# Infini-attention beside a Fourier mixing: where SyncE issues the row loads of the next head group, and where the transposing transfer

## The chip, the cores and the metric

The kernel runs on one core of a Trainium2 chip. The metric is the device time of one execution in microseconds (us), as the median of repeated runs. A core has five engines that matter here: TensorE (PE, matmuls; PEld is its weight load), VectorE (DVE), ScalarE (ACT), GpSimd (POOL) and SyncE (SP). In this kernel SyncE does nothing but issue the transfers (DMAs), in the order of the program.

## The reference, cut to what matters

Two independent results stand side by side in the output. A is an attention with a compressive memory over 2048 rows of width 576, with 32 heads of 18 and four segments of 512 rows; B is a Fourier mixing, two matrix products along the width and two along the sequence.

```python
# A, for each of the 4 segments
p = softmax(qs @ ks.T * scale + causal_mask)      # 512 x 512 per head
a_dot = p @ vs
a_mem = (phi(qs) @ M) / (phi(qs) @ z + 1e-6)
o = g * a_mem + (1 - g) * a_dot
M, z = M + phi(ks).T @ vs, z + phi(ks).sum()
out_A = o_all @ wo
# B
a, b = x @ dft_hid_re.T, x @ dft_hid_im.T
out_B = dft_seq_re @ a - dft_seq_im @ b
```

## The kernel before, in words

Full precision is kept by splitting: a float32 operand becomes a rounded high part and the low remainder, and a product becomes three matmuls.

There are three stages. The first (lines 435 to 479) goes through the segments: `project_qk` and `project_v` make queries, keys and values, `lookup` and `accumulate` read and write the memory. Queries and keys are stored in DRAM (`qd`, `kd`) as three bf16 parts each, values as `vd`. The second stage holds two streams at once. `attention()` (line 805) does the softmax attention of A as 68 steps `p` of eight pieces; after each piece it yields a share of time (`SLOTS`), and the loop at line 867 fills that share on TensorE with matmuls of `dense()` (line 573), which is B: 16 tiles of `hidden` and 16 of `sequence` for the real part, then the same for the imaginary part. The third stage multiplies the attention's output by `wo`.

The instructions of every engine are issued in the order in which this program emits them; nothing reorders them later. `later(n, fn)` (line 82) puts a call `n` ticks ahead, and a tick falls after each piece, so that a load is issued that many pieces later.

Heads go in groups of four. `stack_load(G)` (line 420) brings the rows of group `G` from DRAM: twelve transfers, six into `qs` and six into `ks`, each for one of the bf16 parts, spread over three ticks (`each=2`), or over six ticks for the first group (`each=1`), and `lag` ticks later the group's values, `vst`. There are four buffers for the rows of a group. In `attention()` group `G` is loaded by the step `p = 2G - 2`, and its first scores (`s_fill`, line 673, the matmul at line 664) stand at the opening of step `p = 2G`. A matmul of scores reads all the parts of a head, so it needs all twelve transfers.

Even and odd heads take different ways. For an even head the row maxima are found first, transposed by TensorE (`maxima_transpose`, line 719), written to DRAM (`md`) and read back into three more rows of `qs` (line 725); then scores are computed a second time in transposed form (`t_fill`, line 727) with the maxima as part of the product. For an odd head the exponentials `f` are split into `hl` by ACT (line 700), POOL and DVE (line 704), and one transposing transfer (`f_turn`, line 706, the DMA at line 709) turns `hl` into `ptt`, with two buffers, which `pv` (line 765) multiplies with the values. There is one such transfer per step.

SyncE waits at each issue for what the transfer needs. Each transfer signals on one of eight semaphores, taken in turn, and the issue of a transfer also waits for the one that used its semaphore before, eight places back.

Before the change `stack_load(p // 2 + 1)` is called in the first piece of an even step, and `f_turn` at the end of the last piece of each step. On SyncE the twelve rows so stand behind the transposing transfer of the odd step before, with the store `md` between them, and the load of `md` into `qs` stands behind the rows. The first group's call stands at `n == 6` of the last segment's loop over the projections (line 462), so that its last pair is issued in the last of the four value blocks.

The quoted functions follow.

## Time and profile before

| | |
|---|---|
| median of 3 runs | 1030.98 us (1029.33 to 1032.97) |
| the profiled execution | 1030.27 us, its span 1028.5 us |
| VectorE, ScalarE, GpSimd busy | 69%, 70%, 61% |
| transfers of SyncE's queue | 73.5% of the 16 engines' span, 192.81 MB |
| transposing transfers | 64 |
| row loads | 384, of 72 KB each |

A line of the page's list of groups or waits names the line of the kernel, the engine and the tile that is written and read (`s<-ks,qs` is a matmul into `s`). "A <- B" in a list of waits says that A waited for B. In a timeline the first figure is the start in us from the start of the span and the second the length; an idle time ahead of the instruction stands in brackets with what ended it; x2 says that two are merged. For a transfer the timeline shows the time that SyncE spends on the issue, not the landing; the chain of waits shows the time to the landing where a landing is part of the chain. In a table of windows each row gives the window, its length, the busy time of PE, PEld, DVE, ACT and POOL, the granted clock of TensorE (1.00 is full), the DMA engines' busy share and GB/s.

### The profile page before, as it was taken

The page shows a single profiled execution, that of the slowest core. Times are in us where ns is not written, and L with a number is a line of the kernel's source. Part 1 is how long each engine was busy: PE and PEld are TensorE (multiplying, and loading weights), DVE is VectorE, ACT ScalarE, POOL GpSimd, SP SyncE. Part 2 cuts the span into 40 slices and gives each one's busy share as a digit, 9 for nine tenths or more (in the row PEclk, how much of TensorE's full clock was granted, in tenths as well). Part 3 has the DMA queues.
Part 4 walks back from the last instruction along what each step waited for, and adds up shares of the span by engine and source line. Part 5 has one row for each costly group of instructions (what it writes and reads, how often), then busy time and mean ns, then how long its engine had stood idle before and what let it go on. Part 6 is the DMA issues. An engine that isn't in the chain of part 4 may idle for free.

```text
span 1028.5 us, 25886 instructions
## 1 busy us (share of the span) xinstructions
PE 1007.7 (98%) x9464; PEld 942.5 (92%) x9464; DVE 705.9 (69%) x1903; ACT 715.0 (70%) x1654; POOL 624.2 (61%) x668
## 2 busy tenths in 40 slices
PE   9999999989999999999999999999999999999998
PEld 7989989889999999998998999999999889999998
DVE  6645557563677777778888777777777778885442
ACT  6657575653777787877878788877677777876333
POOL 2657575775666677676766867666667567666000
PEclk9999999998999999999999999999999999999999
DMA  7516243375568887898998987689998899977574
GB/s 250 186 65 204 88 159 147 128 242 151 154 157 190 199 207 197 210 218 193 221 215 194 217 188 182 164 202 226 224 217 195 202 242 234 235 176 182 156 209 137
DMA packets 287743, 194.46 MB, mean 189 GB/s; under 512 B 210496, under 2 KB 242816, under 8 KB 287616
## 3 DMA queue, kind: packets, MB, share of 16 engines
q1 hardware_dynamic: 287616, 192.81, 73.5%
q8 instruction: 74, 1.21, 0.5%
q14 instruction: 53, 0.43, 0.1%
HBM read 106.84 MB, written 43.97 MB: 147 GB/s over the span
## 4 chain that ended last, share of the span: by engine, by line
PE 83%; DMA 7%; ACT 2%; POOL 2%; DVE 2%; SPq 2%; issue 1%; POOLq 0%; ACTq 0%; DVEq 0%
PE d L493 31%; PE qk L78 6%; PE s L664 6%; PE d L78 6%; PE qk L230 5%; PE v L78 4%; PE pv L780 4%; PE d L539 3%; PE d L540 3%; PE d L541 3%; DMA qs<-md 2%; PE pv L781 2%; PE m L314 2%; DMA ptt<-hl 2%; DMA ks<-kd 2%; PE look L339 1%
## 5 line engine op out<-in xcount | busy, mean ns | idle before, releaser
L670 DVE CUSTOM_DVE_ANT_0 s<-s,causal 128x128 f32<-128x128 f32 (+3 forms) x512 | 251.7, 498 | 119.9 <-PE s L664 108.6
L393 POOL TENSOR_TENSOR clo<-craw,chi 128x512 fp32r<-128x512 f32 x158 | 209.6, 1327 | 161.4 <-ACT chi L388 128.1
L493 PE MATMUL d<-wide,chi 128*128 128x288 f32 x1408 | 266.7, 306 | 0.0
L493 PEld LDWEIGHTS d<-wide,chi 128*128 128x128 f32 x1408 | 212.3, 189 | 1.3 <-issue 0.2
L493 PE MATMUL d<-wide,clo 128*128 128x288 f32 x704 | 178.0, 319 | 0.0
L664 PE MATMUL s<-ks,qs 108*128 108x128 bf16 (+3 forms) x512 | 134.2, 304 | 6.7 <-DMA ks<-kd 4.3
L704 POOL TENSOR_TENSOR hl<-pf,hl 128x768 f16<-128x768 f32 x64 | 110.2, 1723 | 48.5 <-ACT hl L700 39.8
L693 ACT ACTIVATE pf<-s,nb 128x128 f32<-128x128 f32 (+3 forms) x256 | 128.3, 527 | 6.2
L493 PE MATMUL d<-ab,chi 128*128 128x288 f32 x640 | 126.1, 306 | 0.0
L748 ACT ACTIVATE phi<-t 128x384 f16<-128x384 f32 x128 | 62.3, 487 | 83.7 <-PE t L745 83.7
L493 PEld LDWEIGHTS d<-wide,clo 128*128 128x128 f32 x704 | 119.0, 189 | 1.0
L388 ACT ACTIVATE chi<-craw 128x512 fp32r<-128x512 f32 x160 | 100.6, 630 | 8.1 <-DMA craw<-cT 3.3
L763 DVE TENSOR_TENSOR plo<-pf,phi 128x384 f16<-128x384 f32 (+1 forms) x128 | 105.0, 821 | 0.0
L749 ACT ACTIVATE pf<-t 128x384 f32<-128x384 f32 (+1 forms) x192 | 100.1, 521 | 3.8 <-PE t L738 3.7
L493 PEld LDWEIGHTS d<-ab,chi 128*128 128x128 f32 x640 | 98.5, 189 | 0.4
L700 ACT ACTIVATE hl<-pf 128x768 f16<-128x768 f32 (+1 forms) x128 | 87.4, 729 | 2.0
L539 PE MATMUL d<-wide,chi 128*128 128x288 f32 x256 | 85.6, 334 | 0.0
L493 PE MATMUL d<-ab,clo 128*128 128x288 f32 x320 | 84.9, 314 | 0.0
L540 PE MATMUL d<-wide,chi 128*128 128x288 f32 x256 | 76.5, 299 | 0.0
L541 PE MATMUL d<-wide,clo 128*128 128x288 f32 x256 | 76.4, 299 | 0.0
L763 POOL TENSOR_TENSOR plo<-pf,phi 128x384 f16<-128x384 f32 x64 | 61.3, 957 | 11.5 <-ACT pf L749 10.7
L704 DVE TENSOR_TENSOR hl<-pf,hl 128x512 f16<-128x512 f32 x64 | 62.9, 982 | 0.7 <-ACT hl L700 0.5
(196 smaller groups left out, 2522.8 us busy)
## 6 DMA issues: line engine op xcount, KB each, us to landing
craw<-cT SPq DMA_DIRECT2D x128, 256.0 KB
qs<-qd SPq DMA_DIRECT2D x192, 72.0 KB
ks<-kd SPq DMA_DIRECT2D x192, 72.0 KB
craw<-xtT SPq DMA_DIRECT2D x32, 320.0 KB
out<-y SPq DMA_DIRECT2D x31, 288.0 KB
vd<-vs SPq DMA_DIRECT2D x16, 440.0 KB
vst<-vd SPq DMA_DIRECT2D x32, 220.0 KB
qd<-p SPq DMA_DIRECT2D x16, 384.0 KB
```

The lines of the kernel that those rows point to most:

```text
L78: pe.matmul(o, a, b, start=n == 0, stop=n == len(terms) - 1)
L388: act.activation(hi, raw[:, :4], AF.Copy)
L393: engine.tensor_tensor(lo, raw[:, :4], hi.bitcast(F32), OP.subtract)
L493: pe.matmul(o[h], a, b[:, h * 288:h * 288 + 288], start=start, stop=stop)
L539: pe.matmul(o, xh[:, k], wl[k][:, cs], start=k == 0, stop=False)
L540: pe.matmul(o, xh[:, k], wh[k][:, cs], start=False, stop=False)
L541: pe.matmul(o, xl[:, k], wh[k][:, cs], start=False, stop=False)
L664: pe.matmul(o[:, c:c + w], q[:, i * P:w], k[:, :w], start=True, stop=True)
L670: dve.tensor_tensor_reduce(o[:, c:c + w], o[:, c:c + w], CAUSAL[0][:, L - w:], scale=scale, scalar=-LOWEST, op0=OP.add, op1=OP.min, accum_ ...
L693: act.activation(f[:, FIRST_COL[i]:FIRST_COL[i] + w], o[:, c:c + w], AF.Exp, bias=nb[:, i:i + 1], scale=-1.0)
L704: engine.tensor_tensor(hl[:, 1, a:b], f[:, a:b], hl[:, 0, a:b], OP.subtract)
L763: (pool if kind == 2 else dve).tensor_tensor(lo[:, a:b], f[:, a:b], hi[:, a:b], OP.subtract)
```

## The change

Three things are moved, and nothing is added or taken out.

- The first group's rows: the call moves from `n == 6` to `n == 4`, and with it the making of the first pair of buffers (and POOL's fill of one). The loads are issued two ticks sooner.
- The transposing transfer `f_turn` moves from the end of the last piece to the opening of the last but one.
- The rows of the next group are called right behind it, in the seventh piece of an even step instead of its first. The delay of the values' load goes from 39 to 33 ticks, so that it keeps its piece.

On SyncE the rows of a group now follow the transposing transfer of the even step and, for most groups, the load `vst`; the transposing transfer of the odd step comes after them. The maxima's store and load no longer have rows between or ahead of them. The orders of TensorE, VectorE and ScalarE stay the same, and POOL's but for the one fill.

```diff
-    def stack_load(G, lag=39, each=2):
+    def stack_load(G, lag=33, each=2):
...
-            if not more and n in (5, 6):
-                stacks(sr, n - 5)
+            if not more and n == 4:
+                stacks(sr, 0)
+                stack_load(0, 99, 1)
             if not more and n == 5:
                 c_load(0)
             if not more and n == 6:
-                stack_load(0, 99, 1)
+                stacks(sr, 1)
...
-            if p % 2 == 0:
-                stack_load(p // 2 + 1)
             if p % 2 == 0 and 0 < p <= NP:
                 maxima_transpose(p // 2 - 1)
...
             yield SLOTS[5]
+            odd(F_LAG + 1, f_turn)
+            if p % 2 == 0:
+                stack_load(p // 2 + 1)
             odd(V_LAG, pv)
...
             if p >= V_LAG:
                 pv_out(p - V_LAG)
-            odd(F_LAG + 1, f_turn)
             yield SLOTS[7]
```

## The prediction

> **What bounds the kernel now.** I read the page first, then the list of waits of TensorE, then the windows and timelines around the waits, last the chain of waits. The page says that TensorE is the bound:

> ```profile
> span 1028.5 us, 25886 instructions
> ...
> PE 1007.7 (98%) x9464; PEld 942.5 (92%) x9464; DVE 705.9 (69%) x1903; ACT 715.0 (70%) x1654; POOL 624.2 (61%) x668
> ```

> Matmuls fill 1007.7 of 1028.5 us. The change leaves TensorE's order as it is, so it can win only out of the 20.8 us that remain. The list of TensorE's waits divides them (engine, line, what it waited for, total us, times, longest):

> ```profile
> PE s L664 <- DMA ks<-kd: 4.3, 1, 4.3
> PE t L738 <- DMA qs<-md: 3.9, 6, 0.9
> PE pv L780 <- DMA ptt<-hl: 2.4, 2, 1.7
> PE s L664 <- DVE negm L670: 2.3, 3, 0.9
> ...
> PE trm L721 <- POOL mb L717: 1.4, 1, 1.4
> ```

> Three are waits for SyncE's transfers, and each has its part of the change: the first group's rows (4.3 us, once), the maxima rows (3.9) and the transposing transfer (2.4), 10.6 us together. The other two rows are not touched.

> The first wait costs more than its length. In TensorE's timeline it stands ahead of the first scores, and the matmuls behind it run slow:

> ```profile
> 232.06 0.58 PE L664 MATMUL s<-ks,qs 108*128 108x512 bf16 x1 [4.34 <-DMA ks<-kd]
> ...
> 236.76 0.44 PE L540 MATMUL d<-wide,chi 128*128 128x288 f32 x1
> 237.00 0.44 PE L541 MATMUL d<-wide,clo 128*128 128x288 f32 x1
> ...
> 262.24 0.30 PE L540 MATMUL d<-wide,chi 128*128 128x288 f32 x1
> 262.37 0.30 PE L541 MATMUL d<-wide,clo 128*128 128x288 f32 x1
> ```

> The same pair of matmuls starts 0.24 us apart here and 0.13 us apart later. The windows (PEclk is the third figure from the end) show why, and that a wait of 1.7 us, which is the longest one at L780, does not do this:

> ```profile
> 225.00:237.50 12.50, 8.16 (x46) 7.80 (x45) 5.51 (x13) 3.44 (x9) 6.00 (x6) 0.75 0.71 230
> ...
> 825.00:837.50 12.50, 10.81 (x117) 10.04 (x117) 8.93 (x28) 7.43 (x18) 6.94 (x10) 1.00 0.98 239
> ```

> The clock was at half speed for the 5.3 us from 232.1 to about 237.4, which costs 5.3 x (1 - 0.13/0.24) = 2.4 us.

> **Part one, the first group's loads two steps sooner: minus 6.7 us.** Nothing is added; a fill of ks on POOL and twelve row loads (DMAs) move up past the kd stores. SyncE's timeline before:

> ```profile
> 217.84 0.38 SPq L378 DMA_DIRECT2D craw<-xtT  x1
> 218.28 1.11 SPq L88 DMA_DIRECT2D qs<-qd  x1
> ...
> 228.24 0.35 SPq L88 DMA_DIRECT2D ks<-kd  x1
> ```

> The last ks row goes out at 228.24, behind the stores of the third value block. In the new order the last pair stands behind the craw load of 217.84, so it goes out near 219 and should land four to five us later, well before TensorE is free for the first scores (232.06 - 4.34 = 227.7). The 4.3 us and the slow clock's 2.4 us both go. On POOL the fill goes ahead of one subtraction that only a kd store waits for, and those rows are read many groups later. I name nothing that is late next. If the cover fails, no more than the 6.7 us comes back.

> **Part two, the transposing transfer a piece sooner, ahead of the rows: minus 6.3 us.** It is one issue on SyncE per step, and it is long:

> ```profile
> L709 SPq DMA_TRANSPOSE ptt<-hl x64: 3013/3814/5378, 272.1 to 943.7; - x64
> ```

> One period of two steps in SyncE's timeline, then VectorE's two ends of hl in it, then TensorE's scores that open a period:

> ```profile
> 484.10 3.06 SPq L709 DMA_TRANSPOSE ptt<-hl  x1
> ...
> 488.78 0.80 SPq L88 DMA_DIRECT2D qs<-qd  x2
> 489.63 0.83 SPq L88 DMA_DIRECT2D ks<-kd  x2
> 490.55 0.30 SPq L88 DMA_DIRECT2D md<-mt  x1
> ...
> 494.27 0.34 SPq L88 DMA_DIRECT2D od<-og  x1
> ...
> 495.46 0.69 SPq L88 DMA_DIRECT2D ks<-kd  x2
> 496.20 0.75 SPq L88 DMA_DIRECT2D qs<-md  x1
> ...
> 497.53 0.59 SPq L432 DMA_DIRECT2D vst<-vd  x1
> 498.23 4.00 SPq L709 DMA_TRANSPOSE ptt<-hl  x1
> ...
> 505.35 4.53 SPq L709 DMA_TRANSPOSE ptt<-hl  x1
> ```

> ```profile
> 493.23 1.76 DVE L704 TENSOR_TENSOR hl<-pf,hl 128x512 f16<-128x512 f32 x1
> ...
> 504.51 0.69 DVE L704 TENSOR_TENSOR hl<-pf,hl 128x512 f16<-128x512 f32 x1
> ```

> ```profile
> 488.53 0.38 PE L664 MATMUL s<-ks,qs 108*128 108x512 bf16 x1
> ...
> 509.02 0.38 PE L664 MATMUL s<-ks,qs 108*128 108x512 bf16 x1
> ```

> The transfer of 505.35 starts 0.15 us after its data (504.51 + 0.69 = 505.20): it waits for VectorE, and an earlier place in the order gives it nothing. The one of 498.23 had its data at 494.99 and stood 3.2 us behind the rows and the maxima. That half comes sooner, and the late pv (2.4 us) goes. The maxima row at 496.20 stands behind the twelve rows; without them it goes out some 3 us sooner, and the 3.9 us at L738 go too. What it newly waits for is its own store, which the rows used to cover, and behind that wait stand a craw load and the next transposing transfer.

> **Part three, the rows behind the transposing transfer: plus 25 us.** This is the disputed term. No work is added (twelve loads of 72 KB per group, as before), but they lose their lead. Before, the rows of the group that starts at 509.02 went out from 488.78 to 496.15, and 495.83 + 4.1 (below) leaves nine us after landing. Now they start when the transfer that has its data at 494.99 is issued. The chain of waits gives what a landing takes (start, us, what):

> ```profile
> 489.63 4.58 DMA ks<-kd
> ...
> 496.20 4.07 DMA qs<-md
> ...
> 717.00 8.15 DMA ptt<-hl
> ...
> 794.35 3.15 DMA md<-mt
> ```

> A transfer takes one of eight semaphores in turn, and its issue waits until the one eight places ahead has landed: the ks row of 489.63 lands at 494.21, and the eighth issue behind it, od, goes out at 494.27. So, in that period: transposing transfer at 495.1, off SyncE after 4.0 (499.1), vst 0.6 (499.7), eight rows at 0.4. The ninth waits for vst to land, taken at 4 us like the rows (503.1), the last ones for the first rows, so the twelfth goes out near 504.5 and lands 4.1 to 4.6 us later: 508.6 to 509.1, against 509.02. On its own that is a stall of about 0.1 us. But the transposing transfer need not start at 495.1. SyncE now holds, between two such transfers, the rows and two craw loads at the pace of the landings, then the other transposing transfer, then the maxima's store and the wait for it (3.15 us), with only od and a craw load to fill it. That makes it late by 0 to 2 us; I take 1.0, the middle, since neither end has a nearer row. The stall is then 1.1 us per group. It counts in the stretches with a period of 20.5 us (509.02 - 488.53); the hidden products have longer ones, and there the transfers have room (GB/s is the last figure, the DMA share stands before it):

> ```profile
> 385.00:551.00 166.00, 163.79 (x1775) 152.96 (x1773) 131.24 (x372) 131.84 (x307) 111.96 (x114) 1.00 0.88 208
> 593.00:665.00 72.00, 72.00 (x750) 68.27 (x749) 54.17 (x166) 58.72 (x152) 49.11 (x58) 1.00 0.74 178
> 707.00:898.00 191.00, 185.03 (x2002) 172.24 (x2001) 147.59 (x443) 142.49 (x328) 127.67 (x132) 1.00 0.93 221
> ```

> With shares of 0.88 and 0.93 there is little room to catch up. Some 23 of the 32 groups lie in such stretches (all but the first few and those beside the second hidden products): 23 x 1.1 = 25 us. The ends: 0 if every chain comes out under 14 us (a short transposing issue of 3.0 us alone gives 1.0 back), and 23 x 1.9 = 44 us if SyncE is late by most of the 2 us each time.

> [...]

> **The sum.** The profiled execution took 1030.27 us, 0.7 below the median of 1030.98. 1030.3 - 6.7 - 3.9 - 2.4 + 25 = 1042.3 us.

> **The rivals.** *First, on the other side: the rows land in time.* SyncE's one transposing issue in two is shorter when less is queued ahead of it (3.06 at 484.10, 4.00 at 498.23); each us there is a us of margin, and above 0.1 to 1.1 us of it the stalls end. For it: fewer transfers stand between the transposing one and the last row (md and od are gone). Against it: the DMA share. Then 1030.3 - 13.0 = 1017.3 us. *Second, the two cancel:* stalls of 0.6 us per group, 23 x 0.6 = 13: 1030 us. *Third, long stalls slow the clock as the first one did:* if the 11 groups of the later stretch, where the share is 0.93, each stall 4.3 us, they cost 4.3 + 2.4 each, 74 us: 1091 us. Against it: 4.3 us is more than twice the lateness that I allow. [...] *Fourth, that the change does not do what it says* holds for half of the transposing transfers, as shown; it is in the sum.

> **How the numbers follow.** Rows late, about 1042 us: 0.65. In time, 1017: 0.20. Cancelled, 1030: 0.11. Slow clock, 1091: 0.04. A measurement of this kernel can tell about 0.3% (3 us) from no change; so faster 0.20, same 0.11, slower 0.69. The range goes from 1016, the first rival less the spread of runs (1029.33 against the median of 1030.98), to 1061, the forecast with the upper end of the stalls (1017 + 44).

> **What would show it.** Right: the row of s at L664 waiting for qs or ks leads TensorE's waits with 15 us or more in over ten waits, none of them near 230 us; the waits for qs<-md and ptt<-hl are gone; PEclk is 1.00 from 225 us on. The maxima's load on SyncE follows its store by three us or more. Wrong: no such row at L664 (then the first rival, near 1017), or waits at L738 that stay (then md was not held by the rows). A wait at L664 near 230 us would refute part one. What would make the sum wrong is above all the pace of landings once the rows stand elsewhere, which no row of this profile shows.

## The result and the profile after

The changed kernel takes 1061.15 us (median of 4 runs, 1057.41 to 1064.64) against 1031.91 us before (4 runs): ratio 1.029, 95% interval 1.024 to 1.033. The profiled execution took 1057.41 us, 27.1 more than the one of before. It is slower, as forecast, by some two and a half times as much as forecast. Here and below, times and ratios leave out runs more than 1.5% above the fastest of their kernel; two of the kernels had such runs. The code below the change stands one line lower (L664 is now L665, L738 is L739). The page of the changed kernel gives span and engines:

```profile
span 1055.7 us, 25951 instructions
...
PE 1015.6 (96%) x9464; PEld 949.7 (90%) x9464; DVE 703.4 (67%) x1903; ACT 716.0 (68%) x1654; POOL 618.9 (59%) x668
```

TensorE's idle time has grown from 20.8 to 40.1 us, and the same matmuls take 7.9 us longer: 19.3 + 7.9 is the whole 27.2 us of the span. Both parts have their place. The list of TensorE's groups has one row for the scores; behind the bar stand busy time, ns of one, idle time ahead of them and what ended it:

```profile
L665 PE MATMUL s<-ks,qs 108*128 108x128 bf16 (+3 forms) x512 | 134.8, 306 | 31.4 <-DMA ks<-kd 8.1 <-DMA craw<-cT 7.1 <-DMA y<-yd 4.2
```

The row had 6.7 us before, 4.3 of them in the first group. Of the 31.4 us, 28.9 stand ahead of the first scores of 19 groups, in TensorE's timeline, 0.2 to 3.3 us each, 1.5 on the mean; no wait stands near 230 us. The releasers that the row names vary (a row, a chunk load, a y load, now and then ScalarE), but in 18 of the 19 groups the scores start within 0.5 us of the landing of the group's last row, as the trace's landings give it; the one left, at 558 us, is 0.2 us long. The waits for qs<-md and ptt<-hl are gone from TensorE's list. SyncE's own list of waits has a new row, which it had not before:

```profile
SPq L88 <- DMA md<-mt: 27.0, 25, 2.2
```

One period of SyncE's timeline, with VectorE's end of hl and TensorE's opening scores from theirs:

```profile
839.34 4.14 SPq L710 DMA_TRANSPOSE ptt<-hl  x1
843.54 0.58 SPq L432 DMA_DIRECT2D vst<-vd  x1
844.18 0.88 SPq L88 DMA_DIRECT2D qs<-qd  x2
...
849.26 0.80 SPq L88 DMA_DIRECT2D ks<-kd  x2
850.35 0.36 SPq L378 DMA_DIRECT2D craw<-cT  x1
850.89 4.90 SPq L710 DMA_TRANSPOSE ptt<-hl  x1
855.84 0.57 SPq L378 DMA_DIRECT2D craw<-cT  x1
856.51 0.34 SPq L88 DMA_DIRECT2D md<-mt  x1
```

```profile
838.57 0.69 DVE L705 TENSOR_TENSOR hl<-pf,hl 128x512 f16<-128x512 f32 x1
```

```profile
855.30 0.38 PE L665 MATMUL s<-ks,qs 108*128 108x512 bf16 x1 [1.05 <-ACT pf L694]
```

VectorE ends at 839.26, the transposing transfer starts 0.08 us later, the rows follow at once, and the last one lands at about 855.0: 15.7 us from the transfer's start, and 1 us too late. That is the chain of part three.

The longer matmuls come from the clock. Windows of the changed kernel, of 3.41 us (the DMA share passes 1 in windows as short as these):

```profile
828.60:832.02 3.42, 0.23 (x2) 0.23 (x3) 1.46 (x2) 2.72 (x6) 0.91 (x2) 1.00 1.24 211
832.02:835.43 3.41, 3.41 (x18) 3.26 (x17) 0.76 (x2) 0.99 (x2) 2.61 (x2) 0.50 1.01 185
872.98:876.39 3.41, 1.64 (x29) 1.44 (x28) 2.95 (x10) 2.87 (x8) 1.37 (x2) 1.00 1.23 224
876.39:879.80 3.41, 3.03 (x13) 2.97 (x13) 1.41 (x4) 1.62 (x4) 1.71 (x2) 0.50 1.06 184
804.72:808.13 3.41, 1.94 (x16) 1.73 (x15) 2.63 (x8) 0.00 (x0) 0.34 (x1) 1.00 1.05 252
808.13:811.54 3.41, 3.22 (x27) 2.96 (x26) 1.28 (x5) 2.99 (x7) 2.00 (x2) 1.00 1.33 269
```

With a stall of 3.30 us (it ends at 831.8) and one of 2.15 us (876.8) the clock stood at half for 3.41 us; with one of 1.47 us (807.7) it did not. Six such spells go with six stalls of 2.07 to 3.30 us, at 340.5, 449.7, 763.8, 832.0, 876.4 and 924.2 us. Before there was one, twice as long (231.15 to 237.98), at the first group's wait.

### The profile page after: what moved, and what is told of

It reads as the page before. It is cut to its first block, busy times and chain, and to the rows that moved or that the text cites. A ratio compares the mean times of both kernels' runs of the same rounds, so it can differ in the third digit from the quotient of the medians.

```text
span 1055.7 us, 25951 instructions
## 1 busy us (share of the span) xinstructions
PE 1015.6 (96%) x9464; PEld 949.7 (90%) x9464; DVE 703.4 (67%) x1903; ACT 716.0 (68%) x1654; POOL 618.9 (59%) x668
## 4 chain that ended last, share of the span: by engine, by line
PE 75%; DMA 10%; ACT 4%; SPq 4%; POOL 3%; DVE 2%; issue 1%; POOLq 0%; ACTq 0%; DVEq 0%
PE d L494 26%; PE qk L78 6%; PE d L78 6%; PE s L665 6%; PE qk L230 5%; PE v L78 4%; DMA ks<-kd 4%; PE d L540 3%; PE d L541 3%; PE d L542 3%; DMA craw<-cT 3%; PE pv L781 3%; DMA qs<-qd 2%; PE m L314 2%; SPq L88 2%; SPq L710 2%
## 5 line engine op out<-in xcount | busy, mean ns | idle before, releaser
L494 PEld LDWEIGHTS d<-wide,chi 128*128 128x128 f32 x1408 | 216.7, 192 | 1.3 <-issue 0.2
L665 PE MATMUL s<-ks,qs 108*128 108x128 bf16 (+3 forms) x512 | 134.8, 306 | 31.4 <-DMA ks<-kd 8.1
L388 ACT ACTIVATE chi<-craw 128x512 fp32r<-128x512 f32 x160 | 100.8, 631 | 26.0 <-DMA craw<-cT 16.8
L665 PEld LDWEIGHTS <-qs 108*128 108x128 bf16 x512 | 40.3, 98 | 50.4 <-issue 19.0
L540 PE MATMUL d<-wide,chi 128*128 128x288 f32 x256 | 84.4, 330 | 0.0
L541 PE MATMUL d<-wide,chi 128*128 128x288 f32 x256 | 75.7, 296 | 0.0
```

The source lines that it names most:

```text
L388: act.activation(hi, raw[:, :4], AF.Copy)
L494: pe.matmul(o[h], a, b[:, h * 288:h * 288 + 288], start=start, stop=stop)
L540: pe.matmul(o, xh[:, k], wl[k][:, cs], start=k == 0, stop=False)
L541: pe.matmul(o, xh[:, k], wh[k][:, cs], start=False, stop=False)
L665: pe.matmul(o[:, c:c + w], q[:, i * P:w], k[:, :w], start=True, stop=True)
```

## The experiments

Every ratio is against the kernel before on the same chip, with its 95% interval; a difference between two of the kernels is that of their ratios, in us of 1031. The first theory was that of the prediction: the rows have lost their lead, and SyncE's blocked wait for the maxima's store makes the transposing transfer ahead of them late. The rivals change with what the runs showed.

### The parts alone

*Part one alone* (the first group's loads sooner; the rest as before).

> The kernel before with part one alone: the first group's rows two steps sooner, all else as before. By the sum of the prediction the wait of 4.3 us at the first scores and the half clock behind it (2.4 us) go: 6.7 us less than before, ratio 0.9935, and the waits at L738 and L780 stay. If the first group's sooner loads only crowd the stores of kd and of the values, the time stays within 2 us of before and a wait of another kind stands near 230 us.

1026.83 us, 0.996 (0.995 to 0.998). Its page and its list of waits:

```profile
PE 1005.2 (98%) x9464; PEld 940.8 (92%) x9464; DVE 704.1 (69%) x1903; ACT 714.6 (70%) x1654; POOL 622.4 (61%) x668
```

```profile
PE t L739 <- DMA qs<-md: 6.8, 6, 2.6
```

The first wait is gone, and in the profiled run the clock never fell; without a half-clock spell the matmuls take 1005.2 us, 2.5 less than before (2.4 had been worked out). But the maxima's waits rose from 3.9 to 6.8 us, and some 4 us of the 6.7 remain.

*The transposing transfer a piece sooner alone*, the rows in their old place:

```diff
             yield SLOTS[5]
+            odd(F_LAG + 1, f_turn)
             odd(V_LAG, pv)
...
-            odd(F_LAG + 1, f_turn)
             yield SLOTS[7]
```

> The kernel before with part two alone: the transposing transfer a piece sooner in the order, the rows still called in the first piece of the even step. My theory (it is the rows' place that costs, not the transposing transfer's): half of these transfers wait for VectorE anyway, the other half stay behind the rows and the maxima; within 3 us of before, waits at the scores only the first one of 4.3 us. A rival, that the transposing transfer's sooner place holds up what follows it on SyncE (its issue waits for hl with everything behind it): 10 us slower or more.

1035.96 us, 1.005 (1.003 to 1.008): slower. In its list of waits the pv wait halved and the maxima's grew by more:

```profile
PE t L738 <- DMA qs<-md: 9.8, 9, 2.7
...
PE pv L780 <- DMA ptt<-hl: 1.2, 1, 1.2
```

### More lead for the rows, same place in the step

*Rows two steps sooner* in the changed kernel:

```diff
-            if p % 2 == 0:
+            if p in (0, 2):
                 stack_load(p // 2 + 1)
+            elif p == 3:
+                stack_load(3, 41)
+            elif p % 2 == 0:
+                stack_load(p // 2 + 2, 49)
```

> The changed kernel with the rows at the same place of the step but two steps (one group) sooner, so SyncE's order has the same pattern and the same load between the transposing transfers; only the lead grows by some 21 us. If the loss is the lost lead, the waits at the scores and the half clock behind them go, and so do those for the maxima and the transposing transfer: 13 us less than before, about 1018 us, ratio 0.987. If the loss is SyncE blocked by the wait for the maxima's store, or the order of the transfers on the DMA engines, both are still there, and the time stays over 1040 us, with the waits moved to the maxima or to ptt.

1051.1 us, 1.019 (1.016 to 1.023). No row is late any more, and yet only 10 of the 30 us come back. Its waits, TensorE's and ScalarE's:

```profile
ACT chi L388 <- DMA craw<-cT: 35.0, 19, 5.9
...
PE t L742 <- ACT mt L724: 13.4, 5, 3.8
...
PE s L665 <- ACT pf L694: 3.6, 3, 3.0
```

ScalarE waits for the other stream's chunk loads (16.8 us in the changed kernel), TensorE for ScalarE, and five half-clock spells stand in the trace. SyncE is still blocked 30.2 us for the maxima's store. So the lead is not the whole of it.

*Rows one step sooner*, behind the odd step's transfer, with the maxima behind them:

```diff
-            if p % 2 == 0:
+            if p in (0, 2):
                 stack_load(p // 2 + 1)
+            elif p % 2 and p > 1:
+                stack_load((p + 3) // 2, 41)
```

> The changed kernel, but the rows go behind the transposing transfer of the odd step, one step sooner: they gain 10 us of lead, and the maxima's store and load stand behind the rows again, with nothing long between. Theory (what costs is the place of the rows behind the even step's transfer: it leaves them no lead, and everything that SyncE issues behind them, the odd step's transfer, the maxima's store and the chunk loads of the other stream, comes late too): the waits at L665 for rows are gone, ScalarE waits for chunk loads for less than 8 us (16.8 in the changed kernel), the waits for the maxima are 4 to 10 us as with either other part alone, and the time is 1027 to 1037 us. Rival (the loss comes from the transposing transfer being issued sooner, or from the rows meeting it on the DMA engines, whichever of the two it is): 1045 us or more.

1069.54 us, 1.039 (1.036 to 1.042). The time is the rival's, the cause is neither's, for the maxima's waits grew:

```profile
PE t L739 <- DMA qs<-md: 29.3, 18, 4.7
```

All twelve rows now go out ahead of the maxima's store, whose landing SyncE then waits for with nothing to issue (71.0 us in its list). In the old order four rows go out first and the others while the store is under way.

*The maxima's load behind the even step's transfer*, so that SyncE isn't blocked for the store (`later(4, ...)` in `maxima_transpose` becomes `later(7, ...)`).

> The changed kernel with the maxima's load three pieces later, so that it stands behind the transposing transfer of the even step and SyncE no longer stands blocked for the maxima's store ahead of it (27 us in the changed kernel's list of SyncE's waits, 25 times). If that blocked wait makes the chain late (the second half of my part three), the transposing transfer and the rows start some 1 us sooner each time, and about 20 us of the 29 us of waits at the scores go, with new short waits for the maxima at L739: about 1040 us. If it is the lead alone, by far the most of the loss stays: 1055 us or more.

1078.27 us, 1.047 (1.044 to 1.050). The row waits fall to 2.9 us and the maxima's take their place:

```profile
PE t L739 <- DMA qs<-md: 43.4, 28, 2.9
```

### The maxima without the trip through DRAM

In four kernels the maxima rows go straight from their tile into qs, by two transfers in place of two (the rows of `mb` are put in the order head, part, tile for it):

```diff
-        later(1, dma, md[G], w)
-        later(4, dma, qs_bufs[G % 4][NPAIR:NPAIR + 3, 0:4:2], md[G].rearrange("(c h n) t -> c h (n t)", c=3, h=2))
+        for h in range(2):
+            later(1, dma, qs_bufs[G % 4][NPAIR:NPAIR + 3, 2 * h], w[12 * h:12 * h + 12])
```

*In the changed kernel:*

> The changed kernel, but the maxima rows go straight from their tile into qs by two transfers, with no trip through DRAM, so that SyncE never waits for their store (27.0 us in the changed kernel). Theory (the stall is a chain that runs from VectorE's end of hl through the transposing transfer, vst and the twelve rows to their landing; in the changed kernel that transfer starts within 0.1 to 1.1 us of its data, so the blocked wait adds little to it): the row waits at L665 fall by no more than 0.5 us each, 1045 to 1058 us. Rival (the blocked wait makes that transfer late by 1.0 us, as the prediction put it): the waits fall to about 0.5 us each, no half-clock spell is left, 1035 us or less.

1049.56 us, 1.018 (1.014 to 1.022): 11 us of the loss come back. The row waits, in the list of groups, fall by 5.8 us, and three half-clock spells are left of six:

```profile
L665 PE MATMUL s<-ks,qs 108*128 108x128 bf16 (+3 forms) x512 | 134.0, 304 | 25.6 <-DMA craw<-cT 7.4 <-DMA ks<-kd 5.7 <-ACT pf L694 4.1
```

*With the rows one step sooner:*

> The kernel with the rows one step sooner (1069.5 us; 29.3 us of waits for the maxima, 38.7 us of ScalarE's for chunks), with the maxima rows sent directly. Theory (there the maxima's store goes out only behind the twelve rows, and its trip, 4.2 us to land and 2.1 more for the load, is exposed): the waits at L739 fall below 8 us, 1030 to 1045 us. Rival (SyncE is crowded at that place, whichever transfers stand there): 1055 us or more.

1036.02 us, 1.006 (1.004 to 1.008), 34 us less than with the trip. Of its waits:

```profile
ACT chi L388 <- DMA craw<-cT: 46.2, 28, 4.1
...
PE t L740 <- DMA qs<-mt: 1.5, 2, 1.3
```

So the exposed trip of the maxima was most of the loss there. And the largest wait for chunks of these kernels, 46.2 us, goes with one of the shorter times: ScalarE's wait for chunks is no measure of the loss.

*With the rows two steps sooner:*

> The kernel with the rows two steps sooner (1051 us; no row late, but ScalarE waits 35 us for chunk loads and TensorE 20 us behind it), with the maxima rows sent directly. Theory (the chunk loads are late because SyncE stands blocked for the maxima's store, 30.2 us, and because the rows are issued in one run between the transposing transfers; the first share goes): ScalarE's waits for chunks fall to 10 to 25 us, 1030 to 1045 us. Rival (the blocked wait has no part in it): 1048 us or more. Second rival (it is all of it): 1028 us or less.

1045.0 us, 1.013 (1.009 to 1.017): the upper end of the theory's range, but ScalarE's waits for chunks did not fall (35.5 us), so the way that it named is not the one.

*In the old order, with part one:*

> The kernel before with the first group's rows sooner (1026.8 us), with the maxima rows sent directly. Theory (in the old order the trip of the maxima through DRAM is the tightest of SyncE's chains): the 6.8 us of waits at L739 are gone and nothing takes their place, 1017 to 1022 us. Rival (what stands behind the maxima in the order is as late): 1025 us or more.

1033.25 us, 1.003 (1.001 to 1.005), 7 us slower than with the trip. The maxima's waits are gone, pv waits 9.5 us for ptt instead, and in the later stretch the transposing issue takes 4.5 us on the mean in place of 4.1.

### The place of the rows, and the place of the scores

*Rows ahead of the even step's transfer*, three pieces sooner; all else as in the changed kernel:

```diff
             yield SLOTS[2]
+            if p % 2 == 0:
+                stack_load(p // 2 + 1, 36)
...
             odd(F_LAG + 1, f_turn)
-            if p % 2 == 0:
-                stack_load(p // 2 + 1)
             odd(V_LAG, pv)
```

> The changed kernel, with the transposing transfer where the change puts it, but the rows called three pieces sooner, so that they stand ahead of the even step's transfer in SyncE's order; the maxima's store and load stay ahead of them. Theory (the stalls come from the rows' place behind that transfer, 4.7 us of issue and its wait for VectorE): no row is late, the six half-clock spells are gone, and what is left is the transfer some 3 us behind its data, which pv has time for: 1022 to 1032 us. Rival (the rows anywhere between the maxima's load and the next store crowd SyncE, as with the rows two steps sooner): chunk loads late, 1040 us or more.

1040.69 us, 1.009 (1.006 to 1.012): 20 of the 30 us are back. The run whose profile was taken had no half-clock spell and took 1034.19 us, the other six 1040.0 to 1043.7 at a mean clock of 0.993 to 0.995 (1.000 in the profiled one), which speaks for some. Its waits, then, are those of the fastest run:

```profile
ACT chi L388 <- DMA craw<-cT: 23.6, 11, 4.5
...
PE pv L781 <- DMA ptt<-hl: 9.7, 9, 2.6
...
PE s L665 <- ACT pf L694: 6.9, 5, 3.1
```

No row is late (from the third group on the rows land 4.6 us or more ahead). The transfer, now behind the rows, is late instead.

*The opening scores one piece later on TensorE*, nothing moved on SyncE (`even(0, s_fill, 0)` goes from the first piece to the end of the second).

> The changed kernel with the scores that open a step computed one piece later on TensorE, behind the first two transposed ones: some 2 us more for the rows to land, nothing else moved. Theory (the chain from VectorE's hl to the last row's landing is too long by 0.2 to 3.3 us, 1.5 on the mean, and the longer stalls bring the half clock on): the row waits fall from 28.9 to under 8 us, at most one half-clock spell stays, 1028 to 1038 us. Rival (the chain closes on itself: what TensorE gains, VectorE's next hl takes, or the maxima become late): 1048 us or more.

1055.7 us, 1.023 (1.019 to 1.027): the rival. Its groups:

```profile
L665 PE MATMUL s<-ks,qs 108*128 108x128 bf16 (+3 forms) x512 | 133.3, 304 | 8.7 <-DMA ks<-kd 4.3 <-DMA craw<-cT 3.2 <-DVE negm L671 1.0
...
L739 PE MATMUL t<-qs,ks 111*128 111x128 bf16 x256 | 25.5, 223 | 9.3 <-ACT pf L694 9.3
```

The row waits fall as expected, but waits for ScalarE at L739 (9.3) and L742 (6.2) come up in their place, and the steps are hardly shorter: from 717 us on the groups start 22.3 us apart, 22.8 in the changed kernel and 21.1 before. That the chain from VectorE's hl to the rows to the scores to the next hl closes on itself is the rival's reading; it fits, but no run isolates it.

### The chunk loads off SyncE

In six kernels the chunk loads (`c_load`, from the sixth on) are issued by another engine, three times by ScalarE, three times by GpSimd:

```diff
-            dma(t[:, :k], src[at])
+            (act.dma_start if n > 4 else dma)(t[:, :k], src[at])
```

*ScalarE: the changed kernel; rows two steps sooner; the old order with part one.*

> The changed kernel with the chunk loads issued by ScalarE. Theory: the row waits at L665 get shorter by the 0.8 us that two chunk loads take between two transposing transfers, from 1.5 us each to 0.5 to 1.0, fewer half-clock spells (0 to 3 in place of 6), 1035 to 1048 us. Rival (the rows land late because of the DMA engines, not because of SyncE's order): 1055 us or more.

> The kernel with the rows two steps sooner (1051 us), but the chunk loads of the other stream (craw) are issued by ScalarE, a queue of their own. In the kernel with them on SyncE no row was late any more, yet ScalarE waited 35 us for chunks, up to 5.9 us at a time. Theory (those late chunks hold up ScalarE's exponentials and by them TensorE): the waits for chunks fall below 8 us, TensorE's waits at L742 and for pf (20 us together) to under 5, the clock stays at 1.00, and the time is 1025 to 1036 us. Rival (the load of SyncE or of the DMA engines as such, or the maxima behind the odd step's transfer): the waits move to the maxima or to ptt, 1043 us or more.

> The kernel before with the first group's rows sooner (1026.8 us), and the chunk loads issued by ScalarE. Theory: SyncE has 0.8 us less to issue per step, the maxima come sooner, the 6.8 us of waits for them fall below 3: 1020 to 1025 us. Rival (the 0.8 us per step on ScalarE, busy 70%, delay the exponentials by as much): 1027 us or more.

1099.25 us, 1.068 (1.065 to 1.072); 1100.25 us, 1.070 (1.065 to 1.075); 1112.11 us, 1.080 (1.075 to 1.084). All far slower: on the side of the rivals, and by more than either side had named. SyncE's waits in the last one:

```profile
SPq L88 <- DMA craw<-cT: 81.7, 40, 5.5
```

With part one alone this row has 3.1 us (10 times). The transfers at L88 neither read nor write a chunk, so SyncE here waits for semaphores that chunk loads signal on, and ScalarE now issues those at its own time. The test says nothing on late chunks; it was made again with GpSimd (`pool.dma_start`), where that wait comes to 0.5 us in the first kernel.

*GpSimd: the old order with part one; the changed kernel; rows two steps sooner.*

> The kernel before with the first group's rows sooner (1026.8 us), and the chunk loads issued by GpSimd, the engine that releases their buffers. With ScalarE as the issuer SyncE waited 82 us for chunk loads, whose semaphores its own transfers share (1112 us). Theory (what harmed there was that sharing, not the second queue as such; GpSimd's transfers have semaphores of their own): no wait of SyncE for a chunk is left, SyncE's issue has 0.8 us less per step, the waits for the maxima fall below 3 us, 1019 to 1026 us. Rival (two queues at once slow the transposing transfers, or GpSimd, busy 61%, is late with the low parts): 1040 us or more.

> The changed kernel with the chunk loads issued by GpSimd. Theory (rows and chunk loads are late together because both stand in one queue behind the transposing transfer; two chunk loads stand between that transfer and the last row): ScalarE's waits for chunks (16.8 us) are gone, the row waits fall by the 0.8 us of two issues each, 1036 to 1050 us. Rival (as with ScalarE as the issuer): 1055 us or more.

> The kernel with the rows two steps sooner (1051 us, no row late, ScalarE waits 35 us for chunks), the chunk loads issued by GpSimd. Theory (the late chunks are what holds up ScalarE and by it TensorE): no waits for chunks, 1024 to 1036 us. Rival (the chunk loads' lateness is only where the wait is booked, and GpSimd or the transposing transfers take their place): 1045 us or more.

1077.37 us, 1.047 (1.040 to 1.054); 1100.74 us, 1.067 (1.064 to 1.070); 1065.54 us (two runs), 1.036 (1.028 to 1.044). The rival's time each time. Waits of the first one, TensorE's:

```profile
PE pv L781 <- DMA ptt<-hl: 31.6, 11, 7.0
...
PE t L739 <- DMA qs<-md: 16.3, 13, 4.0
```

and SyncE's in the second, where the blocked wait has nearly tripled:

```profile
SPq L88 <- DMA md<-mt: 77.1, 30, 5.2
```

The chunks are not what is late now (ScalarE waits 9.3 us for them in the second, 16.8 in the changed kernel; in the first 4.1 us, 1.9 with part one alone), but everything that SyncE issues is: in the first, from 330 to 950 us, a row lands 4.5 us after its issue (median; 3.6 with part one alone), the maxima's store 4.8 (3.2), the transposing transfer 7.8 (6.1). No run here tests apart why they take longer. The first kernel's other rival, GpSimd late with the low parts, is not seen: its part of hl ends 2.9 us ahead of VectorE's in the median, 2.4 with part one alone.

### A version that might beat both

*The maxima's store ahead of the rows, their load ahead of the last four*, in the old order with part one (the calls of `maxima_transpose` and `stack_load` change places, `later(4, ...)` becomes `later(3, ...)`).

> The kernel before with the first group's rows sooner (1026.8 us, 6.8 us of waits for the maxima), and the maxima's store put ahead of the twelve rows, their load ahead of the last four. Theory (in the old order the tightest chain is the maxima's trip, and the rows beside it have nine us to spare): the store goes out 1.6 us sooner, the load some 2 to 3 us, the waits at L739 are gone, 1018 to 1023 us. Rival (the load then stands blocked for its store, and the transposing transfer behind it and the rows comes late instead): 1025 us or more.

1028.37 us, 0.997 (0.995 to 0.999): the maxima's waits are gone, pv waits 7.0 us for ptt instead. Part one alone, 1026.83 us, can't be told from it by these intervals; no other of these kernels is as fast.

## Why the prediction was right and wrong

**The sign was right, and so was the place of the waits.** The scores that open a group wait for rows that have lost their lead, no wait stands near 230 us, and the waits for qs<-md and ptt<-hl are gone. Two of its signs failed: the clock did not stay at 1.00, and the maxima's load follows its store by 2.4 us in the median, not by three or more. What was off most is the size: 1057.41 us profiled against 1042.3. The difference of 15.1 us divides, to 0.1, so: 3.9 in the row stalls (28.9 against 25), 1.0 in other idle time (11.2 against the 10.2 that were to stay of 20.8), and 10.3 in the clock.

**The step that failed is the third rival's condition, and with it the clock in the sum.** The prediction let long stalls slow the clock only at 4.3 us, on two rows (1.7 us harmless, 4.34 not), and took the clock as full from 225 us on. Here stalls of 2.07 to 3.30 us halved it six times. The sum had 1007.7 - 2.4 = 1005.3 us of matmuls; the changed kernel has 1015.6, and the kernel with part one alone, which has no such spell, has 1005.2. So six spells cost 10.4 us, 1.7 each. They needed no 4.3 us in every group: with a mean of 1.5 us, stalls that spread up to 3.3 us were enough here. A mean stall, as I used it, hides that. (The prediction's own reading of the first spell was short as well: behind the wait it lasted 5.9 us, from 232.06 to 237.98, not 5.3.)

**Part three** forecast 23 stalls of 1.1 us, 25 us; 19 of 1.5 us came, 28.9. Its two terms were sized wrongly against each other. The transposing transfer ahead of the rows was to start 1.0 us behind its data because of SyncE's blocked wait: it started 0.5 us behind on the mean, 0.15 in the median of the 23 groups. The chain from its start to the last landing was to take 13.5 to 14.0 us: it took 14.7 on the mean, 12.9 to 16.6, and 15.7 in the period shown, where the second of the last pair goes out at 849.80 and lands at 855.0, 5.2 us later and not 4.1 to 4.6. The pace of landings, which the prediction named as its weakest point, was it. The blocked wait does have a part: without it (the direct maxima) 11 us come back, 5.8 of them in the row waits and 5.4 in the matmuls (1015.6 to 1010.2), though the transposing transfer ahead of the rows starts only some 0.2 us sooner behind its data.

**Part one** was right where it points and too large. Its wait and its clock spell go; alone it brings some 4 us of the 6.7, since 2.9 us come up at the maxima. "I name nothing that is late next" was the gap.

**Part two** took both waits for gains of their own. Alone, the earlier transfer makes the kernel some 5 us slower. The waits that vanish in the whole change vanish because the rows have left the place ahead of the maxima, which is what part three pays for.

**What the experiments settle.** The rows' place behind the even step's transfer costs 20 of the 30 us: ahead of it, with all the rest of the change kept, they come back. The other ten (some 13, as part one's gain is in that kernel) go with part two: the earlier transfer alone costs some 5, and the transfers and chunk loads that are late in that kernel the rest, as far as its waits tell. No run moves the rows alone, with the transfer in its old place, so this division is argued and not shown. More lead at the same place wins back only 10 us, and scores one piece later 6. I had held the lost lead to be the whole mechanism: that fell, since with no row late 20 of the 30 us stayed. What holds in all of these kernels is that SyncE's one queue carries four chains of little slack (rows, maxima, transposing transfer, chunks), and that an order which frees one makes another late. What remains open is why rows two steps sooner with direct maxima still cost 13 us: its waits name ScalarE behind chunk loads, but both attempts to take those off SyncE brought a loss of their own, and the kernel with the rows one step sooner waits longer for chunks and is faster.

## What to carry to other kernels

Before a transfer is moved in a full queue, list for each chain on the queue how long ahead of its use it lands, and price the move by the chain with the least. A load that stands in front of a dependent pair of transfers may be what covers the wait between them (here 27.0 us of blocked waits came up when the rows had gone); see what is left to issue there when it goes. Size stalls by their spread and not by their mean, because only the long ones cost the clock here (2.07 to 3.30 us in the changed kernel, with a mean of 1.5).
